# Adding the three taps of a depthwise convolution with accumulating DMA transfers instead of vector adds

## Chip, cores, metric

One core of a Trainium2 chip. The metric is device time in microseconds (us), median of several executions; the executions of one kernel agree within 0.3% to 1.5%. Engines: PE (matrix), DVE (vector), ACT (scalar activation), POOL (GpSimd), SP (queue for transfers).

## What is computed

The reference, cut to what matters. `B=2, T=16000, D=512`, all bfloat16:

```python
z = zeros_like(x)
for i in range(3):                       # depthwise conv over time, rounded to bf16 after each add
    z = z + xp[:, i:i+T, :] * dw_enc[i]
z = silu(z); res = z
for s in range(4):                       # residual quantizer, 8 codes per stage
    d2 = res.res - 2*res.cb + cb.cb;  idx = d2.argmin(-1)
    q = q + cb[idx];  res = res - cb[idx]
y = second depthwise conv of q with dw_dec
```

The two sums of the first convolution are each rounded. The kernel reproduces that rounding, because an argmin follows.

## The kernel before

Time is cut into 18 tiles of 1792 rows; D is cut into 4 chunks of 128. So a *chunk* below is one 128x1792 block, 4 per tile. A *tap* is one of the three products of a chunk, a *gate* the last DVE instruction of its front, and a transfer has *landed* when its completion is signalled to those who wait for it. Every tile passes four stages (front, select, residual, back), and stages of different tiles are interleaved. The parts that matter here:

```python
def load(st):                            # 14 transposing transfers per tile, SP queue, 2 buffers XT
    for g in list(range(G)):
        nc.sync.dma_start_transpose(out=X[:, :, g + 1, :], in_=src[g])
    ...
def taps(st, i):                         # chunk i: three products, two rounded adds, exponential
    for k in range(K):
        t = ppool.tile([P, R], BF16, name=f"P{k}")          # 3 buffers each
        nc.vector.tensor_scalar(out=t, in0=X[...k...], scalar1=WENC[:, i, k:k + 1], op0=ALU.mult)
        pk.append(t)
    nc.vector.tensor_tensor(out=pk[0], in0=pk[0], in1=pk[1], op=ALU.add)
    nc.vector.tensor_tensor(out=pk[0], in0=pk[0], in1=pk[2], op=ALU.add)
    nc.scalar.activation(pk[1], pk[0], ACT.Exp, scale=-1.0)
def plus1(st, i): ...                    # DVE +1, then ACT Ln and ACT Exp: 1/(1+exp(-z))
def gate(st, i): ...                     # DVE: z * sigmoid(z) into ZB (3 buffers)
...
def update(st, s, i, u, on_act):         # 24 per tile: residual minus chosen codes, in PSUM
    ... matmuls ...
    if on_act: nc.scalar.copy(zg, v)                       # 18 of 24
    else:      nc.vector.tensor_tensor(out=zg, in0=zg, in1=v, op=ALU.add)   # 6 of 24
...
def store(st): ...                       # one whole-tile output buffer, stores issued from GpSimd
```

The text gives a program order. The build step then chooses the order of instructions on each engine (the *built order*).

Of the kernel before, what the change touches and what calls it, by code (L numbers as in the profile page):

```python
# [8 lines left out]
BF16 = mybir.dt.bfloat16  # L9
F32 = mybir.dt.float32  # L10
U16 = mybir.dt.uint16
ALU = mybir.AluOpType
ACT = mybir.ActivationFunctionType
# [4 lines left out]
def kernel(  # L18
# [13 lines left out]
    nc = tc.nc  # L32
    P = nc.NUM_PARTITIONS
# [4 lines left out]
    KT = D // P  # L38
# [12 lines left out]
    const = ctx.enter_context(tc.tile_pool(name="const", bufs=1))  # L51
    ppool = ctx.enter_context(tc.tile_pool(name="ppool", bufs=3))
    lpool = ctx.enter_context(tc.tile_pool(name="lpool", bufs=2))
    selp = ctx.enter_context(tc.tile_pool(name="selp", bufs=2))
    small = ctx.enter_context(tc.tile_pool(name="small", bufs=3))
    ypool = ctx.enter_context(tc.tile_pool(name="ypool", bufs=2))
    psA = ctx.enter_context(tc.tile_pool(name="psA", bufs=3, space=bass.MemoryType.PSUM))
# [7 lines left out]
    make_identity(nc, IDENT)  # L65
    ONES = const.tile([P, P], BF16, name="ONES")
    nc.vector.memset(ONES, 1.0)

# [6 lines left out]

    WENC_b = const.tile([P, KT, K], BF16, name="WENC_b")
    WDBC = const.tile([P, K, D], BF16, name="WDBC")

    CB4 = const.tile([P, D], BF16, name="CB4")
    CB1 = const.tile([NC, D], BF16, name="CB1")  # L80
    wd_rows = bass.AP(tensor=dw_dec.tensor, offset=dw_dec.offset, ap=[[0, P], [D, K], [1, D]])
# [11 lines left out]

    CBT = const.tile([P, KT, NC], BF16, name="CBT")
    CBM2 = const.tile([P, KT, NC], BF16, name="CBM2")
    for i in range(KT):
# [23 lines left out]
    for i in range(KT):  # L120
        nc.tensor.matmul(pg[0:NC, 0:NC], lhsT=CBT[:, i, :], rhs=CBT[:, i, :],
                         start=(i == 0), stop=(i == KT - 1))
    GR = const.tile([NC, NC], F32, name="GR")
    nc.vector.tensor_copy(GR, pg[0:NC, 0:NC])
    NPART = 3
    GP = const.tile([NC, NPART, NC], BF16, name="GP")
    GREM = const.tile([NC, NC], F32, name="GREM")
    nc.vector.tensor_copy(GP[:, 0, :], GR)
# [7 lines left out]
    CCB = const.tile([P, 1, NC], BF16, name="CCB")  # L136
    CCD = const.tile([NC, NPART, NC], BF16, name="CCD")
    nc.vector.tensor_tensor(out=CCD, in0=GP, in1=IDENT[0:NC, 0:NC].rearrange("p (o c) -> p o c", o=1).to_broadcast([NC, NPART, NC]),
# [8 lines left out]

    GM = const.tile([GC, G, 1], F32, name="GM")
    nc.vector.tensor_reduce(out=GM[:, :, 0], in_=IDENT[0:GC, 0:GC].rearrange("p (g c) -> p g c", c=C), axis=AX.X, op=ALU.add)
    BD = {}  # L150
    for s in range(2):
        SEL = const.tile([NC, G, C], BF16, name=f"SEL{s}")
        nc.vector.tensor_copy(SEL, IDENT[0:NC, s * C:(s + 1) * C].rearrange("p (o c) -> p o c", o=1).to_broadcast([NC, G, C]))
        RP = const.tile([GC, NPART, NC], F32, name=f"RP{s}")
        pr = psS.tile([P, 512], F32, name="pr", tag="pss")
        nc.tensor.matmul(pr[0:GC, 0:NPART * NC], lhsT=SEL.rearrange("p g c -> p (g c)"),
                         rhs=GP.rearrange("p q c -> p (q c)"), start=True, stop=True)
        nc.vector.tensor_scalar(out=RP.rearrange("p q c -> p (q c)"), in0=pr[0:GC, 0:NPART * NC], scalar1=2.0,
                                scalar2=None, op0=ALU.mult)
        for s2 in range(s + 1, 3):  # L160
            for q in range(NPART):
                t = const.tile([GC, G, C], BF16, name=f"BD{s}_{s2}_{q}")
                nc.vector.tensor_tensor(out=t, in0=RP[:, q:q + 1, s2 * C:(s2 + 1) * C].to_broadcast([GC, G, C]),
                                        in1=GM.to_broadcast([GC, G, C]), op=ALU.mult)
                BD[s, s2, q] = t
# [4 lines left out]
    for j in range(4):  # L170
        t = const.tile([P, 1], F32, name=f"JM{j}")
        nc.vector.tensor_reduce(out=t, in_=idv[:, :, j, :], axis=AX.XY, op=ALU.add)
        JM.append(t)
# [3 lines left out]
    for v, tp in enumerate(((0, 1, 2, None), (None, 0, 1, 2), (None, None, 0, None), (None, 2, None, None))):  # L177
        w = const.tile([P, D], BF16, name=f"WDEC{v}")
        acc = None
        for j, k in enumerate(tp):  # L180
            if k is None:
                continue
            t = const.tile([P, D], BF16, name=f"WJ{j % 2}")
            nc.vector.tensor_scalar(out=t, in0=WDBC[:, k, :], scalar1=JM[j], scalar2=None, op0=ALU.mult)
            if acc is not None:
                nc.vector.tensor_tensor(out=t, in0=t, in1=acc, op=ALU.add)
            acc = t
        nc.vector.tensor_tensor(out=w, in0=CB4, in1=acc, op=ALU.mult)
        WDEC.append(w)

    CBN = {}
    for s in range(3):
        for u in range(2):
# [5 lines left out]
            CBN[s, u] = w  # L199

    NOH = 4
    PADC = 2
# [5 lines left out]
    for t in KEY:  # L208
        k16 = t.bitcast(U16).rearrange("p g (c h) -> p g c h", h=2)
        for c in range(C):  # L210
            nc.gpsimd.memset(k16[:, :, c, 0], c)


# [18 lines left out]
    def taps(st, i):  # L232
        X = XT[st["n"] % NX]
        pk = []
        for k in range(K):
            t = ppool.tile([P, R], BF16, name=f"P{k}")
            nc.vector.tensor_scalar(out=t, in0=X[:, i, k:k + G, :].rearrange("p g c -> p (g c)"),
                                    scalar1=WENC[:, i, k:k + 1], scalar2=None, op0=ALU.mult)
            pk.append(t)
        nc.vector.tensor_tensor(out=pk[0], in0=pk[0], in1=pk[1], op=ALU.add)  # L240
        nc.vector.tensor_tensor(out=pk[0], in0=pk[0], in1=pk[2], op=ALU.add)  # L241
        nc.scalar.activation(pk[1], pk[0], ACT.Exp, scale=-1.0)  # L242
        st["pk", i] = pk

    def plus1(st, i):
        pk = st["pk", i]
        nc.vector.tensor_scalar(out=pk[1], in0=pk[1], scalar1=1.0, scalar2=None, op0=ALU.add)
        LN = lpool.tile([P, R], F32, name="LN")
        nc.scalar.activation(LN, pk[1], ACT.Ln)
        nc.scalar.activation(pk[1], LN, ACT.Exp, scale=-1.0)  # L250

    def gate(st, i):
        pk = st["pk", i]
        Z = ZB[st["n"] % NZ]
        nc.vector.tensor_tensor(out=Z[:, i, :, N3:N3 + P], in0=pk[0].rearrange("p (g c) -> p g c", c=P),  # L255
                                in1=pk[1].rearrange("p (g c) -> p g c", c=P), op=ALU.mult)

# [113 lines left out]
    def update(st, s, i, u, on_act):  # L371
# [13 lines left out]
        else:  # L385
            nc.vector.tensor_tensor(out=zg, in0=zg, in1=v, op=ALU.add)  # L386

    def decode(st, k):
        W = OHW[st["n"] % NOH]
        if k == 0:  # L390
            st["Y"] = ypool.tile([P, G, D], BF16, name="Y")
        Y = st["Y"]
        py = psA.tile([P, 1024], F32, name="py", tag="psa")
        for u in range(2):
# [5 lines left out]
            elif wrap:  # L400
                nc.tensor.matmul(o, lhsT=W[:, 0, PADC + 1:PADC + 1 + P], rhs=WDEC[3], start=False, stop=True)
        nc.scalar.copy(Y[:, 2 * k:2 * k + 2, :].rearrange("p g d -> p (g d)"), py)  # L402
        if k == GH - 1:
            store(st)

    def store(st):

# [3 lines left out]
        for p in range(P):  # L411
            lo = max(a - G * p, 0)
            hi = min(e - G * p, G)
            if lo >= hi:
                continue
            if runs and runs[-1][2:] == [lo, hi]:
                runs[-1][1] = p + 1
            else:
                runs.append([p, p + 1, lo, hi])
# [4 lines left out]
        for p0, p1, lo, hi in split:  # L424
            nc.gpsimd.dma_start(out=view[p0:p1, lo:hi, :], in_=Y[p0:p1, lo:hi, :])  # L425


    def front(st):
        for j in range(KT + 2):
            if j < KT:  # L430
                yield lambda j=j: taps(st, j)
            if 1 <= j <= KT:
                yield lambda j=j: plus1(st, j - 1)
            if j >= 2:
                yield lambda j=j: gate(st, j - 2)

# [9 lines left out]
    def resid(st):  # L446
        m = 0
        for s in range(3):
            for u in range(2):
                for i in range(KT):  # L450
                    yield lambda s=s, i=i, u=u, m=m: update(st, s, i, u, m % 4 != 3)
                    m += 1
# [10 lines left out]
    NT = len(tiles)  # L463
    order = []
    for n, st in enumerate(tiles):
        order.append((n - 1.0, 0, lambda st=st: load(st)))
        for off, dur, gen in ((0.0, 1.0, front), (1.05, 0.55, select), (1.6, 1.0, resid), (2.6, 0.8, back)):
            w = list(gen(st))
            order += [(n + off + dur * (j + 0.5) / len(w), off, f) for j, f in enumerate(w)]
    for _, _, f in sorted(order, key=lambda t: t[:2]):  # L470
# [31 lines left out]
```

## Time and profile before

| | before |
|---|---|
| median | 889.0 us (887.43 to 890.19) |
| busy | DVE 739.6, ACT 736.1, PE 631.2 of 888.2 us |
| distance of two tiles (first gate to first gate) | 44.3 us |
| busy per period of 44.3 us | ACT 40.75, DVE 39.97, PE 34.97 |

The page's first part (engine, busy us, share of the span, x instructions) and the head of its chain that ended last:

```profile
span 888.2 us, 12372 instructions
...
PE 631.2 (71%) x4660; PEld 358.7 (40%) x4711; DVE 739.6 (83%) x1526; ACT 736.1 (83%) x667; POOL 79.7 (9%) x143
...
q1 hardware_dynamic: 137088, 33.06, 21.7%
q0 software_dynamic: 3840, 32.77, 11.8%
...
DVE 39%; ACT 29%; PE 22%; issue 5%; SPq 3%; DMA 1%; ACTq 0%; POOL 0%; POOLq 0%; DVEq 0%
```

The q lines are queues: packets, MB, share of the time of 16 DMA engines. Here q1 is the loads and q0 the stores. Hardly any of the chain is DMA.

Three consecutive periods of the kernel before, cut at first gates. Columns are in the first line:

```profile
core 0: us, PE busy (x) PEld busy (x) DVE busy (x) ACT busy (x) POOL busy (x), PEclk, DMA share, GB/s
296.60:340.90 44.30, 34.94 (x260) 19.75 (x261) 40.04 (x81) 40.73 (x38) 4.11 (x6) 0.92 0.39 84
340.90:385.30 44.40, 35.04 (x262) 19.89 (x263) 39.87 (x82) 40.82 (x38) 4.29 (x6) 0.92 0.40 84
385.30:429.60 44.30, 34.93 (x260) 19.73 (x261) 40.01 (x81) 40.71 (x38) 3.52 (x6) 0.92 0.39 84
```

Two engines are over 90% busy in every period, and about 3.6 us per period are lost. The DVE timeline (start us, length us) shows what an add and a DVE update cost when the engine is full, 1.00 us from start to start:

```profile
414.33 1.07 DVE L240 TENSOR_TENSOR P_4146<-P_4146,P_4148 128x1792 bf16<-128x1792 bf16 x1
415.33 1.07 DVE L386 TENSOR_TENSOR ZB_138<-ZB_138,pu 128x896 bf16<-128x896 bf16 x1
416.33 1.08 DVE L241 TENSOR_TENSOR P_4146<-P_4146,P_4150 128x1792 bf16<-128x1792 bf16 x1
```

### The profile page before, as it was taken

The numbers are of one execution on the slowest core, as the hardware profiler recorded it, in microseconds if no ns is written. First come the engines' busy times: TensorE is split into PE (matmuls) and PEld (weight loads), VectorE is DVE, ScalarE is ACT, GpSimd is POOL, SyncE is SP. The second block draws the span as 40 slices with busy tenths as digits, with TensorE's granted clock in tenths as the row PEclk, the third lists the DMA queues.
The fourth block names the chain that finished last, engine by engine and source line by source line (L and its number), as shares of the span: only waits on it lengthen the run. The fifth ranks groups of instructions, "written<-read, shape, count | busy, mean of one in ns | idle before, by whom it ended". The sixth has DMA issues, their size and how long they took to land.

```text
span 888.2 us, 12372 instructions
## 1 busy us (share of the span) xinstructions
PE 631.2 (71%) x4660; PEld 358.7 (40%) x4711; DVE 739.6 (83%) x1526; ACT 736.1 (83%) x667; POOL 79.7 (9%) x143
## 2 busy tenths in 40 slices
PE   1003587878787877777878787878787878778892
PEld 0002253535353535353535353535353535444540
DVE  4499999898989898989898989898989898984731
ACT  0076797989898989898989898989898989997572
POOL 5000000101010101010101010101010100000000
PEclk9998698989898989898989898989898989999997
DMA  4412322343434343434343534333534342020213
GB/s 96 95 30 59 78 46 39 94 74 92 75 94 73 96 71 97 70 100 67 99 68 99 68 97 66 103 65 100 67 99 67 98 69 78 7 84 1 84 51 112
DMA packets 143021, 67.20 MB, mean 76 GB/s; under 512 B 139932, under 2 KB 140572, under 8 KB 140700
## 3 DMA queue, kind: packets, MB, share of 16 engines
q1 hardware_dynamic: 137088, 33.06, 21.7%
q0 software_dynamic: 3840, 32.77, 11.8%
q10 hardware_dynamic: 2032, 0.56, 0.3%
q8 instruction: 37, 0.61, 0.3%
q14 instruction: 24, 0.20, 0.1%
HBM read 0.56 MB, written 32.77 MB: 38 GB/s over the span
## 4 chain that ended last, share of the span: by engine, by line
DVE 39%; ACT 29%; PE 22%; issue 5%; SPq 3%; DMA 1%; ACTq 0%; POOL 0%; POOLq 0%; DVEq 0%
PE pu L380 9%; PE pu L379 7%; ACT ZB_139 L384 6%; ACT ZB_137 L384 5%; ACT Y L402 5%; ACT ZB_138 L384 5%; SPq L228 3%; DVE ZB_137 L255 2%; DVE ZB_138 L255 2%; DVE ZB_139 L255 2%; PE pgr L270 2%; PE py L397 2%; DVE M L324 1%; DVE ZB_138 L386 1%; DVE ZB_139 L386 1%
## 5 line engine op out<-in xcount | busy, mean ns | idle before, releaser
L402 ACT CAST Y<-py 128x1024 bf16<-128x1024 f32 x126 | 130.6, 1043 | 13.8 <-PE py L397 13.8
L384 ACT CAST ZB_138<-pu 128x896 bf16<-128x896 f32 x108 | 95.9, 932 | 18.5 <-PE pu L380 18.0
L384 ACT CAST ZB_139<-pu 128x896 bf16<-128x896 f32 x108 | 95.6, 933 | 17.2 <-PE pu L380 16.7
L384 ACT CAST ZB_137<-pu 128x896 bf16<-128x896 f32 x108 | 95.7, 935 | 10.5 <-PE pu L380 10.5
L379 PEld LDWEIGHTS <-IDENT 128*128 128x128 bf16 x648 | 65.6, 101 | 77.8 <-issue 18.9
L270 PE MATMUL pgr<-ZB_137 128*128 128x152 bf16 (+1 forms) x672 | 56.4, 232 | 50.7 <-DVE ZB_137 L255 47.7
L379 PE MATMUL pu<-ZB_137,IDENT 128*128 128x512 bf16 (+1 forms) x216 | 81.1, 375 | 9.3 <-ACT ZB_137 L384 8.2
L379 PE MATMUL pu<-ZB_138,IDENT 128*128 128x512 bf16 x216 | 80.6, 373 | 7.8 <-ACT ZB_138 L384 6.7
L379 PE MATMUL pu<-ZB_139,IDENT 128*128 128x512 bf16 x216 | 80.1, 371 | 8.3 <-ACT ZB_139 L384 7.0
L267 PE MATMUL pgr<-MSK,IDENT 128*128 128x456 bf16 (+3 forms) x180 | 61.0, 339 | 23.2 <-ACT ZB_137 L384 4.8
L270 PEld LDWEIGHTS <-ZB_137 128*128 128x128 bf16 x672 | 48.4, 101 | 70.3 <-DVE ZB_137 L255 52.3
L288 DVE TENSOR_REDUCE rr<-pgr 128x6 f32<-128x768 f32 (+1 forms) x54 | 41.9, 775 | 36.2 <-PE pgr L270 36.1
L425 POOL DMA_DIRECT2D out_dram<-Y x66 | 34.1, 521 | 389.6 <-ACT Y L402 389.3
L386 DVE TENSOR_TENSOR ZB_139<-ZB_139,pu 128x896 bf16<-128x896 bf16 x36 | 39.1, 1085 | 27.9 <-PE pu L380 27.7
L386 DVE TENSOR_TENSOR ZB_138<-ZB_138,pu 128x896 bf16<-128x896 bf16 x36 | 39.0, 1083 | 20.5 <-PE pu L380 20.2
L270 PE MATMUL pgr<-ZB_139 128*128 128x152 bf16 (+1 forms) x672 | 53.3, 226 | 3.0 <-ACT ZB_139 L384 2.9
L270 PE MATMUL pgr<-ZB_138 128*128 128x152 bf16 (+1 forms) x672 | 53.6, 226 | 2.5 <-ACT ZB_138 L384 2.5
L270 PEld LDWEIGHTS <-ZB_139 128*128 128x128 bf16 x672 | 46.6, 98 | 18.4 <-issue 9.1
L270 PEld LDWEIGHTS <-ZB_138 128*128 128x128 bf16 x672 | 46.6, 98 | 17.7 <-issue 8.9
L386 DVE TENSOR_TENSOR ZB_137<-ZB_137,pu 128x896 bf16<-128x896 bf16 x36 | 39.0, 1084 | 12.1 <-PE pu L380 11.8
L242 ACT ACTIVATE P_348<-P_346 128x1792 bf16<-128x1792 bf16 x1 | 1.7, 1696 | 43.6 <-DVE P_346 L241 43.6
L380 PEld LDWEIGHTS <-CBN_0_262 128*128 128x128 bf16 x144 | 18.9, 131 | 32.6 <-issue 25.3
(1280 smaller groups left out, 1741.0 us busy)
## 6 DMA issues: line engine op xcount, KB each, us to landing
out_dram<-Y POOLq DMA_DIRECT2D x18, 1568.0 KB, 8.5
out_dram<-Y POOLq DMA_DIRECT2D x14, 196.0 KB, 8.2
XT_164<-in_x_dram SPq DMA_TRANSPOSE x126
XT_165<-in_x_dram SPq DMA_TRANSPOSE x126
out_dram<-Y POOLq DMA_DIRECT2D x30, 12.0 KB, 2.1
out_dram<-Y POOLq DMA_DIRECT2D x2, 210.0 KB, 8.9
WDBC<-in_dw_dec_dram ACTq DMA_DIRECT2D x1, 384.0 KB
CB_94<-in_codebooks_dram ACTq DMA_DIRECT2D x16, 8.0 KB
```

The costliest lines, as they stand in the source:

```text
L228: nc.sync.dma_start_transpose(out=X[:, :, g + 1, :], in_=src[g])
L255: nc.vector.tensor_tensor(out=Z[:, i, :, N3:N3 + P], in0=pk[0].rearrange("p (g c) -> p g c", c=P), in1=pk[1].rearrange("p (g c) -> p g c", ...
L267: nc.tensor.matmul(o, lhsT=IDENT, rhs=MSK[:, 0:nb, c0:c1], start=True, stop=False)
L270: nc.tensor.matmul(o[:, u * w:(u + 1) * w], lhsT=Z[:, i, b0 + u, N3:N3 + P], rhs=Z[:, i, b0 + u, c0:c1], start=False, stop=(u == nb - 1 an ...
L288: nc.vector.tensor_reduce(out=grp(st["rr"], g0, g1)[:, :, :, 0], in_=v[:, :, :, N3:N3 + P], axis=AX.X, op=ALU.max)
L379: nc.tensor.matmul(o, lhsT=IDENT, rhs=zg[:, k0:k0 + nk, :], start=True, stop=False)
L380: nc.tensor.matmul(o, lhsT=CBN[s, u][:, i * P:(i + 1) * P], rhs=W[:, k0:k0 + nk, PADC:PADC + P], start=not on_act, stop=True)
L384: nc.scalar.copy(zg, v)
L386: nc.vector.tensor_tensor(out=zg, in0=zg, in1=v, op=ALU.add)
L397: nc.tensor.matmul(o, lhsT=W[:, k, PADC:PADC + P], rhs=WDEC[u], start=True, stop=not wrap)
L402: nc.scalar.copy(Y[:, 2 * k:2 * k + 2, :].rearrange("p g d -> p (g d)"), py)
L425: nc.gpsimd.dma_start(out=view[p0:p1, lo:hi, :], in_=Y[p0:p1, lo:hi, :])
```

## The change

Intent: take the 8 adds per tile off DVE by letting DMA engines add in SBUF, and use the room on DVE to take 4 of the 18 updates off ACT. To make the latency of two transfers bearable, the front gets more stages in the program (`LAG`, in tiles) and more product buffers (`NB`); the memory comes from freeing setup tensors and from output buffers of 8 row groups instead of 14. Stores move from GpSimd to SP.

```diff
+    BYDMA = (1, 2)
+    NB = (5, 3, 4, 3)                       # buffers of P0, P1, P2, E
+    LAG = (0.01, 0.16, 0.31, 0.41, 0.42, 0.60)
...
         for k in range(K):
-            t = ppool.tile([P, R], BF16, name=f"P{k}")
+            t = ppool.tile([P, R], BF16, name=f"P{k}", bufs=NB[k])
...
-        nc.vector.tensor_tensor(out=pk[0], in0=pk[0], in1=pk[1], op=ALU.add)
-        nc.vector.tensor_tensor(out=pk[0], in0=pk[0], in1=pk[2], op=ALU.add)
-        nc.scalar.activation(pk[1], pk[0], ACT.Exp, scale=-1.0)
+    def add(st, i, k):
+        if k in BYDMA:
+            nc.gpsimd.dma_start(out=pk[0], in_=pk[k], accum_op=ALU.add)
+        else:
+            nc.vector.tensor_tensor(out=pk[0], in0=pk[0], in1=pk[k], op=ALU.add)
+    def expo(st, i):
+        E = ppool.tile([P, R], BF16, name="E", bufs=NB[3])
+        nc.scalar.activation(E, pk[0], ACT.Exp, scale=-1.0)
...
+    NDVE = 10
+    YG = 8
-                    yield lambda ...: update(st, s, i, u, m % 4 != 3)
+                    yield lambda ...: update(st, s, i, u, (m + 1) * NDVE // 24 == m * NDVE // 24)
...
-            nc.gpsimd.dma_start(out=view[p0:p1, lo:hi, :], in_=Y[p0:p1, lo:hi, :])
+            nc.sync.dma_start(out=view[p0:p1, g0 + lo:g0 + hi, :], in_=Y[p0:p1, lo:hi, :])
...
+            t = n + 0.25 * i
+            put(t, taps, st, i)
+            put(t + LAG[0], add, st, i, 1)
+            put(t + LAG[1], add, st, i, 2)
+            put(t + LAG[2], expo, st, i)
+            put(t + LAG[3], plus1, st, i)
+            put(t + LAG[4], inverse, st, i)
+            put(t + LAG[5], gate, st, i)
```

More of the change, by code (lines that the diff above doesn't have):

```diff
@@ L51 @@
     const = ctx.enter_context(tc.tile_pool(name="const", bufs=1))
-    ppool = ctx.enter_context(tc.tile_pool(name="ppool", bufs=3))
-    lpool = ctx.enter_context(tc.tile_pool(name="lpool", bufs=2))
-    selp = ctx.enter_context(tc.tile_pool(name="selp", bufs=2))
-    small = ctx.enter_context(tc.tile_pool(name="small", bufs=3))
-    ypool = ctx.enter_context(tc.tile_pool(name="ypool", bufs=2))
+    setup_pool = tc.tile_pool(name="setup", bufs=1)
+    setup = setup_pool.__enter__()
     psA = ctx.enter_context(tc.tile_pool(name="psA", bufs=3, space=bass.MemoryType.PSUM))
@@ L65 @@
     make_identity(nc, IDENT)
-    ONES = const.tile([P, P], BF16, name="ONES")
+    ONES = setup.tile([P, P], BF16, name="ONES")
     nc.vector.memset(ONES, 1.0)
@@ L74 @@
                                 op0=ALU.mult, op1=ALU.add)
-    WENC_b = const.tile([P, KT, K], BF16, name="WENC_b")
-    WDBC = const.tile([P, K, D], BF16, name="WDBC")
-    CB4 = const.tile([P, D], BF16, name="CB4")
-    CB1 = const.tile([NC, D], BF16, name="CB1")
+    WENC_b = setup.tile([P, KT, K], BF16, name="WENC_b")
+    WDBC = setup.tile([P, K, D], BF16, name="WDBC")
+    CB4 = setup.tile([P, D], BF16, name="CB4")
+    CB1 = setup.tile([NC, D], BF16, name="CB1")
     wd_rows = bass.AP(tensor=dw_dec.tensor, offset=dw_dec.offset, ap=[[0, P], [D, K], [1, D]])
@@ L91 @@
     nc.vector.tensor_copy(WENC, WENC_b)
-    CBT = const.tile([P, KT, NC], BF16, name="CBT")
-    CBM2 = const.tile([P, KT, NC], BF16, name="CBM2")
+    CBT = setup.tile([P, KT, NC], BF16, name="CBT")
+    CBM2 = setup.tile([P, KT, NC], BF16, name="CBM2")
     for i in range(KT):
@@ L122 @@
                          start=(i == 0), stop=(i == KT - 1))
-    GR = const.tile([NC, NC], F32, name="GR")
+    GR = setup.tile([NC, NC], F32, name="GR")
     nc.vector.tensor_copy(GR, pg[0:NC, 0:NC])
     NPART = 3
-    GP = const.tile([NC, NPART, NC], BF16, name="GP")
-    GREM = const.tile([NC, NC], F32, name="GREM")
+    GP = setup.tile([NC, NPART, NC], BF16, name="GP")
+    GREM = setup.tile([NC, NC], F32, name="GREM")
     nc.vector.tensor_copy(GP[:, 0, :], GR)
@@ L136 @@
     CCB = const.tile([P, 1, NC], BF16, name="CCB")
-    CCD = const.tile([NC, NPART, NC], BF16, name="CCD")
+    CCD = setup.tile([NC, NPART, NC], BF16, name="CCD")
     nc.vector.tensor_tensor(out=CCD, in0=GP, in1=IDENT[0:NC, 0:NC].rearrange("p (o c) -> p o c", o=1).to_broadcast([NC, NPART, NC]),
@@ L144 @@
     nc.vector.tensor_copy(CCB[:, 0, :], pc[:, 0:NC])
-    GM = const.tile([GC, G, 1], F32, name="GM")
+    GM = setup.tile([GC, G, 1], F32, name="GM")
     nc.vector.tensor_reduce(out=GM[:, :, 0], in_=IDENT[0:GC, 0:GC].rearrange("p (g c) -> p g c", c=C), axis=AX.X, op=ALU.add)
@@ L151 @@
     for s in range(2):
-        SEL = const.tile([NC, G, C], BF16, name=f"SEL{s}")
+        SEL = setup.tile([NC, G, C], BF16, name=f"SEL{s}")
         nc.vector.tensor_copy(SEL, IDENT[0:NC, s * C:(s + 1) * C].rearrange("p (o c) -> p o c", o=1).to_broadcast([NC, G, C]))
-        RP = const.tile([GC, NPART, NC], F32, name=f"RP{s}")
+        RP = setup.tile([GC, NPART, NC], F32, name=f"RP{s}")
         pr = psS.tile([P, 512], F32, name="pr", tag="pss")
@@ L170 @@
     for j in range(4):
-        t = const.tile([P, 1], F32, name=f"JM{j}")
+        t = setup.tile([P, 1], F32, name=f"JM{j}")
         nc.vector.tensor_reduce(out=t, in_=idv[:, :, j, :], axis=AX.XY, op=ALU.add)
@@ L182 @@
                 continue
-            t = const.tile([P, D], BF16, name=f"WJ{j % 2}")
+            t = setup.tile([P, D], BF16, name=f"WJ{j % 2}")
             nc.vector.tensor_scalar(out=t, in0=WDBC[:, k, :], scalar1=JM[j], scalar2=None, op0=ALU.mult)
@@ L211 @@
             nc.gpsimd.memset(k16[:, :, c, 0], c)
+    setup_pool.__exit__(None, None, None)
+    ppool = ctx.enter_context(tc.tile_pool(name="ppool", bufs=3))
+    lpool = ctx.enter_context(tc.tile_pool(name="lpool", bufs=2))
+    selp = ctx.enter_context(tc.tile_pool(name="selp", bufs=2))
+    small = ctx.enter_context(tc.tile_pool(name="small", bufs=3))
+    ypool = ctx.enter_context(tc.tile_pool(name="ypool", bufs=2))
     tiles = []
@@ L239, in taps, with inverse @@
             pk.append(t)
-        nc.vector.tensor_tensor(out=pk[0], in0=pk[0], in1=pk[1], op=ALU.add)
-        nc.vector.tensor_tensor(out=pk[0], in0=pk[0], in1=pk[2], op=ALU.add)
-        nc.scalar.activation(pk[1], pk[0], ACT.Exp, scale=-1.0)
         st["pk", i] = pk
+    def add(st, i, k):
+        pk = st["pk", i]
+        if k in BYDMA:
[3 more added lines that the diff above has]
+    def expo(st, i):
+        pk = st["pk", i]
+        E = ppool.tile([P, R], BF16, name="E", bufs=NB[3])
+        nc.scalar.activation(E, pk[0], ACT.Exp, scale=-1.0)
+        st["E", i] = E
     def plus1(st, i):
-        pk = st["pk", i]
-        nc.vector.tensor_scalar(out=pk[1], in0=pk[1], scalar1=1.0, scalar2=None, op0=ALU.add)
+        E = st["E", i]
+        nc.vector.tensor_scalar(out=E, in0=E, scalar1=1.0, scalar2=None, op0=ALU.add)
+    def inverse(st, i):
+        E = st["E", i]
         LN = lpool.tile([P, R], F32, name="LN")
-        nc.scalar.activation(LN, pk[1], ACT.Ln)
-        nc.scalar.activation(pk[1], LN, ACT.Exp, scale=-1.0)
+        nc.scalar.activation(LN, E, ACT.Ln)
+        nc.scalar.activation(E, LN, ACT.Exp, scale=-1.0)
     def gate(st, i):
-        pk = st["pk", i]
         Z = ZB[st["n"] % NZ]
-        nc.vector.tensor_tensor(out=Z[:, i, :, N3:N3 + P], in0=pk[0].rearrange("p (g c) -> p g c", c=P),
-                                in1=pk[1].rearrange("p (g c) -> p g c", c=P), op=ALU.mult)
+        nc.vector.tensor_tensor(out=Z[:, i, :, N3:N3 + P], in0=st["pk", i][0].rearrange("p (g c) -> p g c", c=P),
+                                in1=st["E", i].rearrange("p (g c) -> p g c", c=P), op=ALU.mult)
     def gram(st, g0, g1, c0, c1):
@@ L386, in update @@
             nc.vector.tensor_tensor(out=zg, in0=zg, in1=v, op=ALU.add)
+    NDVE = 10
+    YG = 8
     def decode(st, k):
         W = OHW[st["n"] % NOH]
-        if k == 0:
-            st["Y"] = ypool.tile([P, G, D], BF16, name="Y")
+        if 2 * k % YG == 0:
+            st["Y"] = ypool.tile([P, YG, D], BF16, name="Y")
         Y = st["Y"]
@@ L401, in decode, with store @@
                 nc.tensor.matmul(o, lhsT=W[:, 0, PADC + 1:PADC + 1 + P], rhs=WDEC[3], start=False, stop=True)
-        nc.scalar.copy(Y[:, 2 * k:2 * k + 2, :].rearrange("p g d -> p (g d)"), py)
-        if k == GH - 1:
-            store(st)
-    def store(st):
+        h = 2 * k % YG
+        nc.scalar.copy(Y[:, h:h + 2, :].rearrange("p g d -> p (g d)"), py)
+        if h == YG - 2 or k == GH - 1:
+            store(st, 2 * k - h, 2 * k + 2)
+    def store(st, g0, g1):
         Y, r0, a, e = st["Y"], st["row0"], st["a"], st["e"]
@@ L411, in store @@
         for p in range(P):
-            lo = max(a - G * p, 0)
-            hi = min(e - G * p, G)
+            lo = max(a - G * p, g0) - g0
+            hi = min(e - G * p, g1) - g0
             if lo >= hi:
@@ L424, in store @@
         for p0, p1, lo, hi in split:
-            nc.gpsimd.dma_start(out=view[p0:p1, lo:hi, :], in_=Y[p0:p1, lo:hi, :])
-    def front(st):
-        for j in range(KT + 2):
-            if j < KT:
-                yield lambda j=j: taps(st, j)
-            if 1 <= j <= KT:
-                yield lambda j=j: plus1(st, j - 1)
-            if j >= 2:
-                yield lambda j=j: gate(st, j - 2)
+            nc.sync.dma_start(out=view[p0:p1, g0 + lo:g0 + hi, :], in_=Y[p0:p1, lo:hi, :])
     def select(st):
@@ L450, in resid @@
                 for i in range(KT):
-                    yield lambda s=s, i=i, u=u, m=m: update(st, s, i, u, m % 4 != 3)
+                    yield lambda s=s, i=i, u=u, m=m: update(st, s, i, u, (m + 1) * NDVE // 24 == m * NDVE // 24)
                     m += 1
@@ L464, with put @@
     order = []
+    def put(t, f, *args):
+        order.append((t, len(order), lambda: f(*args)))
     for n, st in enumerate(tiles):
-        order.append((n - 1.0, 0, lambda st=st: load(st)))
-        for off, dur, gen in ((0.0, 1.0, front), (1.05, 0.55, select), (1.6, 1.0, resid), (2.6, 0.8, back)):
+        put(n - 1.0, load, st)
+        for i in range(KT):
+            t = n + 0.25 * i
[6 more added lines that the diff above has]
+            put(t + LAG[5], gate, st, i)
+        t = n + 0.75 + LAG[5] + 0.05
+        for dur, gen in ((0.55, select), (1.0, resid), (0.8, back)):
             w = list(gen(st))
-            order += [(n + off + dur * (j + 0.5) / len(w), off, f) for j, f in enumerate(w)]
+            for j, f in enumerate(w):
+                put(t + dur * (j + 0.5) / len(w), f)
+            t += dur
     for _, _, f in sorted(order, key=lambda t: t[:2]):
```

## The prediction

> **What bounds it now.** The busy table gives DVE 739.6 us (83%), ACT 736.1 (83%), PE 631.2 (71%) of 888.2. One tile of 18 passes every 44.3 us (first gates of tiles 3 and 4 start at 163.7 and 207.9 us). By the windows between 225 and 675 us, a period has ACT busy about 40.7 us, DVE 40.0, PE 35. So ACT and DVE bound together; about 3.5 us per period go in hand-overs (chain of waits: DVE 39%, ACT 29%, PE 22%). Some 135 us are fill and drain.
>
> **What the change does, per tile.**
> - 8 DVE adds of 128x1792 leave (1.08 us each in the line listing, 1.00 start to start in the timeline): DVE -8.0 us.
> - Residual updates on DVE go from 6 to 10 of 24: DVE +4.0 (1.00 each, start to start); ACT loses 4 casts of 0.93 us (0.87 start to start): -3.5; PE loses 8 identity matmuls of 0.37: -3.
> - Sum: DVE 40.0 to 36.0, ACT 40.7 to 37.2, PE 35 to 32.
> - 8 accumulating transfers of 448 KB, 144 in all. The Trainium skill ("DMA: Bandwidth & Descriptors", "SWDGE vs HWDGE vs iDMA") says that only GpSimd can issue accumulation; it states no rate, and this trace has none. My estimate: stores moved 32.77 MB in 11.8% of 16 engines' span, 313 GB/s; an accumulation reads two streams, so 2 x 459 KB / 313 GB/s = 2.9 us, plus the 2.1 us to landing of the 12 KB stores: 5 us each. DMA share goes from 34% to 80%. Program order leaves 0.15 tile (6 us) for each: just hidden.
> - Transposes (20 us per tile from release to landing) slow down, perhaps to 30 us, and have about one period: still hidden.
> - Stores move from GpSimd to SP in two parts: the last is smaller, about 3 us less at the end.
> - GpSimd issues 8 transfers per tile instead of 3.7. The skill ("SBUF — State Buffer", "SBUF: two separate sides") says that DVE in a two-port mode and GpSimd lock each other out of a shared port. Here, single taps took 1.08 us instead of 0.67 beside a GpSimd copy. I allow 0.5 us per tile.
> - Gates come 0.35 tile later in program order: +8 to +12 us of fill and drain.
>
> **On the critical path.** ACT stays the busiest engine, so the period shrinks by its 3.5 us, to 40.8 with hand-overs as before. 17 x 3.5 = 59 us less, +10 for fill and drain, -3 for the last store: 889 - 52 = 837 us. Range 812 to 872. Chances: faster 0.84, same 0.09, slower 0.07.
>
> **What would show each step.** First gates 40.8 us apart; ACT and DVE each about 670 us busy, PE about 580; no adds in the taps on DVE; 144 accumulating transfers landing in 4 to 7 us; DMA share 70 to 85%; little of DVE's or ACT's idle time ended by DMA.
>
> **What would make it wrong.** An accumulation several times slower than a copy: above about 5 us of engine time each, 8 of them with loads and stores exceed the period, the exponentials on ACT wait for the second transfer, and DMA binds (950 us or more). GpSimd's queue is in order and waits for the first sum before it issues the second: with a landing above 9 us each pair passes a quarter of a period. Or descriptor writing stalls DVE's taps by over 2 us per tile. The other way, smaller hand-over losses, since all three engines have more slack, would bring 820.

## The result

1088.86 us against 888.25 us for the kernel before on the same chip (4 runs each): ratio 1.2273, 95% interval 1.2209 to 1.2337. The result is correct. A ratio here is the mean time of one kernel's runs over the mean of the other's of the same rounds, so it is not quite the ratio of the medians quoted. Executions over 1.5% slower than the fastest of the same kernel are left out of the means.

The page of the changed kernel, same parts as before. q0 is now the accumulating transfers, q1 loads and stores:

```profile
span 1088.3 us, 12320 instructions
...
PE 645.9 (59%) x4516; PEld 373.8 (34%) x4567; DVE 680.5 (63%) x1454; ACT 679.3 (62%) x595; POOL 167.9 (15%) x221
...
q0 software_dynamic: 20736, 66.07, 34.8%
q1 hardware_dynamic: 142760, 65.83, 29.1%
...
DMA 31%; DVE 28%; issue 14%; PE 11%; SPq 9%; ACT 4%; POOL 2%; ACTq 0%; POOLq 0%; DVEq 0%
```

Three of its periods, columns as before:

```profile
596.30:651.20 54.90, 36.95 (x253) 21.75 (x259) 36.54 (x78) 37.56 (x33) 8.51 (x10) 0.88 0.67 134
651.20:705.60 54.40, 36.50 (x253) 20.63 (x256) 36.41 (x77) 37.80 (x33) 8.50 (x10) 0.87 0.68 134
705.60:760.30 54.70, 36.91 (x253) 21.58 (x259) 36.57 (x77) 37.56 (x33) 8.50 (x10) 0.88 0.66 135
```

The work did fall as predicted: DVE 36.5 us per period (predicted 36.0), ACT 37.6 (predicted 37.2). But a period is 54.7 us, so ACT stands still for 17 us of it and DVE for 18. The DMA engines are not full either: their share is 0.67.

The first gates show where the 200 us lie. Before, they run from 55.7 to 783.0 us, after from 83.3 to 974.2. So the 17 periods cost 890.9 instead of 727.3 us (+164), the fill 28 us more, and the stretch behind the last tile's first gate 9 us more (114.1 instead of 105.2).

Where does DVE stand? Its timeline over 20 us of the changed kernel; the bracket is the idle time before an instruction and what ended it. Line 244 is a tap, 406 an update, 275 a gate:

```profile
548.48 0.68 DVE L244 TENSOR_SCALAR P_4553<-XT_152,WENC 128x1792 bf16<-128x1792 bf16 x1
...
549.61 0.68 DVE L244 TENSOR_SCALAR P_4676<-XT_152,WENC 128x1792 bf16<-128x1792 bf16 x1
550.20 0.68 DVE L244 TENSOR_SCALAR P_4786<-XT_152,WENC 128x1792 bf16<-128x1792 bf16 x1
550.80 1.08 DVE L406 TENSOR_TENSOR ZB_126<-ZB_126,pu 128x896 bf16<-128x896 bf16 x1
554.87 0.69 DVE L244 TENSOR_SCALAR P_4951<-XT_153,WENC 128x1792 bf16<-128x1792 bf16 x1 [2.99 <-DMA P_4553<-P_4555]
555.47 1.08 DVE L406 TENSOR_TENSOR ZB_126<-ZB_126,pu 128x896 bf16<-128x896 bf16 x1
559.04 0.69 DVE L244 TENSOR_SCALAR P_5038<-XT_153,WENC 128x1792 bf16<-128x1792 bf16 x1 [2.49 <-DMA P_4676<-P_4678]
559.64 1.08 DVE L406 TENSOR_TENSOR ZB_126<-ZB_126,pu 128x896 bf16<-128x896 bf16 x1
...
567.02 0.69 DVE L244 TENSOR_SCALAR P_5162<-XT_153,WENC 128x1792 bf16<-128x1792 bf16 x1 [2.76 <-DMA P_4676<-P_4680]
567.63 1.09 DVE L275 TENSOR_TENSOR ZB_125<-P_4303,E 128x1792 bf16<-128x1792 bf16 x1
569.49 0.69 DVE L244 TENSOR_SCALAR P_5271<-XT_153,WENC 128x1792 bf16<-128x1792 bf16 x1 [0.77 <-DMA P_4786<-P_4790]
```

Read it so. Three chunks get their first product together (P_4553, P_4676, P_4786), so six accumulating transfers run in a bunch. Right behind them in DVE's list stand taps of the *next* tile: P_4951 is the second product of a chunk whose P1 buffer is still being read by the transfer P_4553<-P_4555. The tap may write only when that transfer has landed. Updates and the gate stand behind the waiting tap, and PE and ACT wait for those in turn: between 240 and 640 us DVE is idle for 135 us, 82 of them for such landings; ACT never waits for a landing there, but 62 us for PE's part of the updates and 49 us for gates. Only P0 buffers are freed by a gate; P1 and P2 buffers are freed by a landing.

One chunk's life, from the instructions that write or read its first product (at the line's end: first and last start):

```profile
L244 DVE TENSOR_SCALAR P_4553<-XT_152,WENC x1: 680/680/680, 548.5 to 548.5; 128x1792 bf16<-128x1792 bf16 x1
L253 POOL DMA_DIRECT2D P_4553<-P_4555 x1: 1269/1269/1269, 549.7 to 549.7; - x1
L253 POOL DMA_DIRECT2D P_4553<-P_4557 x1: 859/859/859, 555.1 to 555.1; - x1
L260 ACT ACTIVATE E<-P_4553 x1: 1701/1701/1701, 573.6 to 573.6; 128x1792 bf16<-128x1792 bf16 x1
L275 DVE TENSOR_TENSOR ZB_126<-P_4553,E x1: 1092/1092/1092, 598.9 to 598.9; 128x1792 bf16<-128x1792 bf16 x1
```

The program gives it 0.60 tile from tap to gate; it took 50 us. The next bunch of first products starts at 603.5, after the gates of P_4466, P_4553 and P_4676 (596.3 to 599.9) have freed three P0 buffers. The loop is: gates free P0 buffers, three taps, six landings with DVE waiting through them, late updates, late gates.

The 144 transfers landed after 7.5 us in the median (4.2 to 19.6), by the listing of issues. The longest ones are in the fill, beside loads. The first transfers of the three chunks above, issued together, and one issued alone afterwards (KB, us to landing):

```profile
P_4553<-P_4555 POOLq DMA_DIRECT2D x1, 448.0 KB, 5.1
P_4676<-P_4678 POOLq DMA_DIRECT2D x1, 448.0 KB, 8.2
P_4786<-P_4788 POOLq DMA_DIRECT2D x1, 448.0 KB, 9.5
...
P_4949<-P_4951 POOLq DMA_DIRECT2D x1, 448.0 KB, 4.9
```

The second and third of a bunch land late; one alone takes 4.9 us.

### The profile page after: what moved, and what is told of

It is laid out like the page before. It is cut to its first block, busy times and chain, and to the rows that moved or that the text cites. A ratio compares the mean times of both kernels' runs of the same rounds, so it can differ in the third digit from the quotient of the medians.

```text
span 1088.3 us, 12320 instructions
## 1 busy us (share of the span) xinstructions
PE 645.9 (59%) x4516; PEld 373.8 (34%) x4567; DVE 680.5 (63%) x1454; ACT 679.3 (62%) x595; POOL 167.9 (15%) x221
## 3 DMA queue, kind: packets, MB, share of 16 engines
q0 software_dynamic: 20736, 66.07, 34.8%
## 4 chain that ended last, share of the span: by engine, by line
DMA 31%; DVE 28%; issue 14%; PE 11%; SPq 9%; ACT 4%; POOL 2%; ACTq 0%; POOLq 0%; DVEq 0%
SPq L235 9%; PE pgr L290 4%; PE pu L400 3%; DVE ZB_125 L406 3%; DVE ZB_126 L406 2%; DVE E L265 2%; DVE ZB_127 L406 2%; DMA P_387<-P_389 2%; DVE ZB_126 L275 1%; PE pu L399 1%; DVE rr L308 1%; DVE ZB_125 L275 1%; DVE ZB_127 L275 1%; DMA P_4303<-P_4307 1%; ACT Y L426 1%
## 5 line engine op out<-in xcount | busy, mean ns | idle before, releaser
L270 ACT ACTIVATE LN<-E 128x1792 f32<-128x1792 bf16 x72 | 122.7, 1707 | 41.5 <-DVE E L265 41.5
L271 ACT ACTIVATE E<-LN 128x1792 bf16<-128x1792 f32 x72 | 122.1, 1701 | 0.4
L290 PE MATMUL pgr<-ZB_125 128*128 128x152 bf16 (+1 forms) x672 | 63.9, 249 | 92.3 <-DVE ZB_125 L275 91.1
L399 PEld LDWEIGHTS <-IDENT 128*128 128x128 bf16 x504 | 52.0, 103 | 166.3 <-DVE S L309 104.4
L404 ACT CAST ZB_126<-pu 128x896 bf16<-128x896 f32 x84 | 74.9, 918 | 49.3 <-PE pu L400 45.0
L404 ACT CAST ZB_125<-pu 128x896 bf16<-128x896 f32 x84 | 74.4, 912 | 47.3 <-PE pu L400 42.7
L399 PE MATMUL pu<-ZB_125,IDENT 128*128 128x512 bf16 (+1 forms) x168 | 66.5, 396 | 57.7 <-DVE S L309 36.1
L399 PE MATMUL pu<-ZB_126,IDENT 128*128 128x512 bf16 (+1 forms) x168 | 64.5, 385 | 55.5 <-DVE S L309 31.0
L404 ACT CAST ZB_127<-pu 128x896 bf16<-128x896 f32 x84 | 74.6, 916 | 33.6 <-PE pu L400 32.9
L290 PEld LDWEIGHTS <-ZB_125 128*128 128x128 bf16 x672 | 55.7, 110 | 106.7 <-DVE ZB_125 L275 96.0
L399 PE MATMUL pu<-ZB_127,IDENT 128*128 128x512 bf16 (+1 forms) x168 | 63.3, 378 | 39.5 <-DVE S L309 23.5
L287 PE MATMUL pgr<-MSK,IDENT 128*128 128x456 bf16 (+3 forms) x180 | 72.6, 404 | 2.1 <-DVE MSK L70 1.8
L406 DVE TENSOR_TENSOR ZB_127<-ZB_127,pu 128x896 bf16<-128x896 bf16 x60 | 65.0, 1083 | 13.1 <-PE pu L400 12.8
L406 DVE TENSOR_TENSOR ZB_125<-ZB_125,pu 128x896 bf16<-128x896 bf16 x60 | 64.9, 1081 | 8.8 <-PE pu L400 8.6
L406 DVE TENSOR_TENSOR ZB_126<-ZB_126,pu 128x896 bf16<-128x896 bf16 x60 | 64.9, 1081 | 5.9 <-PE pu L400 5.4
L290 PE MATMUL pgr<-ZB_127 128*128 128x152 bf16 (+1 forms) x672 | 67.0, 258 | 1.0 <-DVE ZB_127 L406 0.7
L290 PE MATMUL pgr<-ZB_126 128*128 128x152 bf16 (+1 forms) x672 | 65.1, 253 | 1.5 <-DVE ZB_126 L406 1.0
L290 PEld LDWEIGHTS <-ZB_127 128*128 128x128 bf16 x672 | 59.5, 116 | 12.1 <-issue 6.7
L290 PEld LDWEIGHTS <-ZB_126 128*128 128x128 bf16 x672 | 57.1, 112 | 11.8 <-issue 5.0
L265 DVE TENSOR_SCALAR E<-E 128x1792 bf16<-128x1792 bf16 x72 | 46.4, 645 | 4.2 <-ACT E L260 4.2
```

The source lines that it names most:

```text
L265: nc.vector.tensor_scalar(out=E, in0=E, scalar1=1.0, scalar2=None, op0=ALU.add)
L270: nc.scalar.activation(LN, E, ACT.Ln)
L271: nc.scalar.activation(E, LN, ACT.Exp, scale=-1.0)
L287: nc.tensor.matmul(o, lhsT=IDENT, rhs=MSK[:, 0:nb, c0:c1], start=True, stop=False)
L290: nc.tensor.matmul(o[:, u * w:(u + 1) * w], lhsT=Z[:, i, b0 + u, N3:N3 + P], rhs=Z[:, i, b0 + u, c0:c1], start=False, stop=(u == nb - 1 an ...
L399: nc.tensor.matmul(o, lhsT=IDENT, rhs=zg[:, k0:k0 + nk, :], start=True, stop=False)
```

## Experiments

Theory A: the landings are waited for by engines that execute in order, because the built order puts taps (and exponentials) where the landing has not come yet. Rival B: bytes; accumulation and transposes together are more than the DMA engines can move in a period. Rival C: the rest of the rewrite (stores in SP's queue, longer front).

Every run below was timed in 3 rounds. "DVE for landings" and "ACT for landings" are my sums of the idle times ended by an accumulating transfer that the timelines list between 240 and 640 us of each run. A zero means none is listed; short ones are not listed.

| run | us | ratio to before | landing, median us | DVE for landings | ACT for landings |
|---|---|---|---|---|---|
| changed kernel | 1089 | 1.227 | 7.5 | 82 | 0 |
| e1 both adds on DVE | 914 | 1.029 | none | none | none |
| e2 one add by transfer | 960 | 1.079 | 5.0 | 0 | 0 |
| e3 64 of 1792 columns (wrong result) | 882 | 0.994 | 2.9 | 26 | 0 |
| f4 896 columns (wrong result) | 979 | 1.101 | 4.0 | 37 | 0 |
| e4 plain copy (wrong result) | 947 | 1.067 | 4.8 | 54 | 0 |
| e8 joint product buffer | 959 | 1.080 | 6.0 | 0 | 56 |
| e11 taps held | 999 | 1.124 | 4.7 | 0 | 84 |
| f1 e8 + longer lags | 976 | 1.098 | 5.1 | 0 | 49 |
| f2 longer lags alone | 1083 | 1.220 | 5.9 | 79 | 0 |
| f3 6 updates on DVE | 1105 | 1.246 | 6.3 | 76 | 0 |
| e13 taps and exponentials held | 1066 | 1.199 | 4.8 | 0 | 50 |
| e14 e13 + longer lags | 942 | 1.061 | 5.4 | 0 | 6 |
| g1 e14 with adds on DVE | 979 | 1.102 | none | none | none |
| **g2 joint buffer, longer lags, exponentials held** | **904** | **1.018** | 5.8 | 0 | 0 |

Not in the table: e5, e10, e17 and e18, told below.

### e1: the rest of the change without accumulating transfers

```diff
-    BYDMA = (1, 2)
+    BYDMA = ()
-    NDVE = 10
+    NDVE = 6
```

> Edit: the whole new kernel, but both adds on DVE again and 6 of 24 updates on DVE, as before; buffers, lags, half-tile outputs and stores from SP stay new. Theory A (DVE, in order, waits for landings of the accumulating transfers, because its taps reuse product buffers that a transfer still reads): no landings, so about 890 us (870 to 910), period 44 to 45 us. Rival C (the rest of the rewrite, above all stores ahead of loads in SP's queue and the longer front, costs the time): stays above 1000 us.

Measured 914 us, 2.9% over before (2.7 to 3.1), 4 us outside the expected range. So the transfers and what goes with them are 175 of the 200 us, and the rest of the rewrite costs 25 us that the prediction had only as 10 us of fill. Part of the run is remarkable; two windows of 40 us of e1, columns as before:

```profile
240.00:280.00 40.00, 30.64 (x241) 18.11 (x243) 39.92 (x82) 39.81 (x37) 0.74 (x1) 0.91 0.50 120
440.00:480.00 40.00, 29.57 (x217) 16.30 (x218) 34.14 (x72) 32.77 (x31) 2.37 (x2) 0.91 0.33 76
```

Between 240 and 280 us both DVE and ACT are full; later the same work settles into a period of 48 us with both at 85% or less. I take the built order, which settles into one pattern per period, for the reason; that was not isolated. In the profiled executions (911.6 against 888.2 us) its 17 periods cost 734.2 us together, only 7 more than before, as the first ones are short; 16 us of the loss lie behind the last tile's first gate (120.9 instead of 105.2), which the prediction did not foresee.

### e2: one add by transfer

```diff
-    BYDMA = (1, 2)
+    BYDMA = (2,)
```

> Edit: only the second add by transfer, the first on DVE; 10 updates on DVE as in the changed kernel. DVE work per tile is as before the change, ACT has 3.5 us less. Theory A: half of the landings, no pair in series, so DVE's wait for landings at most half (under 6 us per tile against 11), and 900 to 980 us. Rival B (bytes: accumulation and transposes saturate the DMA engines): landings fall near 5 us and the time near 870. Rival C: above 1000.

960 us, inside A's range, but not by A's route: between 240 and 640 us no wait of DVE for an accumulation is listed. Instead its taps wait 58 us there for loads and stores, and ACT's exponentials 62 us for gates. This run does not tell the theories apart.

### e3, f4 and e4: what a landing is worth

e3 and f4 shorten each transfer, keeping all 144 of them and all waits:

```diff
-            nc.gpsimd.dma_start(out=pk[0], in_=pk[k], accum_op=ALU.add)
+            nc.gpsimd.dma_start(out=pk[0][:, 0:64], in_=pk[k][:, 0:64], accum_op=ALU.add)      # e3; f4: 0:896
```

> Wrong result on purpose: each accumulating transfer adds 64 of 1792 columns; all 144 transfers and their waits stay, 1/28 of the bytes. The built order moves a little. Landing should be 2 to 3 us. If the time of the landing (transfer of bytes) is the cost (A or B): 840 to 880 us. If the mere chain of two transfers through GpSimd's in-order queue is the cost, or rival C: above 1000 us.

> Wrong result on purpose: each accumulating transfer adds 896 of 1792 columns, 224 KB. Landing alone about 3.8 us, between 2.9 (64 columns) and 4.8 (full, uncontended). If the loss follows the landing time: 930 to 1000. If it jumps where bunched transfers overlap: near 882 to 910.

e3: 882 us (2 us over the expected range), with landings of 2.9 us. Its settled periods are 42.5 us (44.4 before, means of twelve): with landings this short about half of the predicted 3.5 us appears, though DVE still loses 26 of 400 us to them. f4: 979 us, inside the range for a loss that follows the landing, with landings of 4.0 us. The number of transfers and GpSimd's queue are the same in all three, so they are not the cost; the loss grows with the length of the landing. The built order moves between these runs, so they are no pure measurement.

e4 has exactly the built order of the changed kernel, on every engine (the lists of all engines in the two traces agree instruction by instruction, semaphore waits left out):

```diff
-            nc.gpsimd.dma_start(out=pk[0], in_=pk[k], accum_op=ALU.add)
+            nc.gpsimd.dma_start(out=pk[0], in_=pk[k])
```

> Wrong result on purpose: the same transfers without accumulation (plain copies, same bytes, same issue, and the built order of all engines is the same). If the read-modify-write is what makes landings slow: landing 3 to 4 us, GpSimd queue share of the DMA engines from 35% to under 20%, and time 900 to 980. If latency and place in the order matter and not the accumulation: landing stays near 7 us and the time within 3% of 1089.

947 us, as forecast: 142 us less, for the same instructions in the same order. (The finer forecasts were missed: landings of 4.8 us instead of 3 to 4, and 22.1% of the engines instead of under 20%.) Its queue of copies and its issues (KB each, median us from issue to landing):

```profile
q0 software_dynamic: 11520, 66.07, 22.1%
...
P<-P POOLq DMA_DIRECT2D x144, 448.0 KB, 4.8
```

An accumulation takes 34.8% of 1088.3 us / 144 = 2.63 us of all 16 engines, a copy 22.1% of 946.2 us / 144 = 1.45 us. (The prediction's estimate for the accumulation was 2.9 us.) With the accumulation's longer occupation a bunch of six lands late: 7.5 us instead of 4.8. In the same order, that difference is 142 us. So neither the choice of engine nor the order alone is the loss; it is a landing time that this order does not tolerate.

### e8 and e11: freeing the buffers otherwise, holding the taps

e8 allocates the three products of a chunk together, so that no buffer is freed by a landing alone (12 product tiles as before):

```diff
-            t = ppool.tile([P, R], BF16, name=f"P{k}", bufs=NB[k])
+        PP = ppool.tile([P, K, R], BF16, name="PP", bufs=4)     # ahead of the loop; t = PP[:, k, :]
```

e11 leaves the buffers and only forbids that taps of a chunk stand ahead of the gate of the chunk three before it:

```diff
+        with (tc.issue_after(GATES[c - 3].ins) if c >= 3 else ExitStack()):
             for k in range(K): ...                              # the three taps
```

> Edit: the changed kernel, the three products of a chunk in one allocation of 4 buffers (same 12 product tiles): the second and third product are freed by the gate and not by a landing. Theory A: the taps stop waiting for landings, as in e11, time 880 to 980. If only bytes matter: above 1040. The fewer chunks in flight (4 instead of 5) may cost some.

> Edit: the changed kernel; only the order on DVE is held: the taps of a chunk may not stand before the gate of the chunk three before it, which is the program's own order. Same instructions, buffers and bytes. Theory A (order): taps no longer stand behind fresh landings, the transfers of a tile spread over it, landing median 5 to 6 us, DVE idle for landings under 4 us per tile (11 in the changed kernel), time 880 to 960. Theory B (bytes saturate the DMA engines): landing stays above 7 us, time above 1040.

e8: 959 us, as A said. e11: 999 us, between the two. In both, DVE's listed waits for landings are gone, from 82 us to zero, and in e11 the landings are back at 4.7 us with the DMA engines' bytes unchanged: with the 4.9 us of a lone transfer in the changed kernel, this says that bunching made them long, not the total. But a new wait appeared. The first exponential on ACT, which reads the finished sum, now stands ahead of its landing, and in e8 DVE stands 57 of 400 us at its +1, waiting for that exponential. Two of its instances in e8's timeline of ACT:

```profile
501.46 1.70 ACT L261 ACTIVATE E<-PP 128x1792 bf16<-128x1792 bf16 x1 [7.33 <-DMA PP<-PP]
...
547.78 1.70 ACT L261 ACTIVATE E<-PP 128x1792 bf16<-128x1792 bf16 x1 [5.83 <-DMA PP<-PP]
```

### f1, f2, f3: lags and the division of updates

```diff
-    LAG = (0.01, 0.16, 0.31, 0.41, 0.42, 0.60)
+    LAG = (0.01, 0.20, 0.50, 0.62, 0.63, 0.82)      # f2 in the changed kernel; f1 in e8
-    NDVE = 10
+    NDVE = 6                                        # f3, in the changed kernel
```

> Edit: e8 (959 us) with the lags of e14 and no held order. e8's remaining waits were ACT's exponentials for the second landing, 7 us per tile. If the place of the exponential in the program is what lets it stand before its landing: those waits fall under 3 us per tile and the time to 895 to 935. If the built order takes no notice of the lags: 950 to 970.

> Edit: the changed kernel with the lags of e14 alone. DVE's taps still wait for landings through the second and third product's buffers, so if those waits are the main cost: 1050 to 1100, DVE idle for landings over 8 us per tile. If the lags are: below 1000.

> Edit: the changed kernel with 6 of 24 updates on DVE as before the change (ACT gets 3.5 us per tile back, DVE loses 4). If updates behind stalled taps on DVE spread the stall to PE and ACT: 1000 to 1060. If the landings' own loop sets the period: within 2% of 1089, as neither DVE nor ACT is full.

f2, 1083 us, as forecast: longer lags alone gain 6 us. The built order moved with them (the list of DVE differs from the changed kernel's), but DVE still waits 79 us for landings. f1, 976 us: a miss of both forecasts, 17 us worse than e8; its ACT still waits 49 us for landings. f3, 1105 us, inside its 2%: giving the four updates back to ACT changes little, since neither engine is full. The shift of updates is not the fault.

### e13, e14, e17, e18, g1: holding the order on both engines

These hold the taps and the first exponential behind the instruction of another stage that precedes them in the program on their engine:

```diff
+        with (tc.issue_after(LAST["v"].ins) if "v" in LAST else ExitStack()):   # ahead of the three taps
+        with (tc.issue_after(LAST["a"].ins) if "a" in LAST else ExitStack()):   # ahead of the first exponential
```

> Edit: the changed kernel; the taps on DVE and the first exponential on ACT of each chunk are held behind the instruction of another stage that precedes them in the program on their engine. Buffers, lags and bytes unchanged. e11 held the taps alone, 999 us, and its wait moved to ACT's exponentials (10 us per tile for landings). Theory A (in-order engines stand before landings that the built order takes to come sooner): ACT's wait for landings under 4 us per tile, time 880 to 950. Rival B (the DMA engines, or GpSimd's chain of two transfers, cannot deliver faster): stays above 980.

> Edit: e13 with longer lags in the program (second transfer 0.20 instead of 0.16 tile after the taps, exponential 0.50 instead of 0.31, gate 0.82 instead of 0.60). Theory A: with 12 us left for each landing nothing waits for a transfer, DVE 36 and ACT 37 us per tile show through, period 41 to 43 us, time 850 to 900. Rival B: no better than e13.

> Edit: e1 (no accumulating transfers, 6 updates on DVE; 914 us) with the same holds as e13. If e1's 25 us over the kernel before are an accident of the built order: 870 to 895. If they come from the longer front and its buffers: 905 or more.

> Edit: e2 (second add by transfer, first on DVE, 10 updates on DVE; 960 us) with the same holds and lags 0.20, 0.40, 0.52, 0.72. DVE has 40 us of work per tile, ACT 37, one landing per chunk. Theory A: 870 to 900, DVE bound. Rival B: bytes half of e14, so clearly faster than e14 and near e2 or below.

> Edit: e14 with both adds on DVE and 6 updates on DVE; same holds and lags. Pair to e14 (942 us). If moving the adds gains once no engine waits for a landing (the prediction's sum of 3.5 to 4 us per tile): 985 to 1010. If the gain is not there: 935 to 955.

My forecasts failed here. e13 took 1066 us instead of 880 to 950; by its time alone that was rival B's forecast (above 980), which e14 then contradicts. e17, the same holds without any accumulating transfer, took 988 us: its second branch (905 or more), but the holds on both engines cost 74 us by themselves (914 without), so it does not say what e1's 25 us are. e18 took 987 us instead of 870 to 900. So theory A as I had it, "keep the program's order and the gain appears", is wrong: e13 gains only 23 us on the changed kernel, and the same holds cost 74 us where there is no landing to wait for.

e14 missed its forecast too (850 to 900). It and e13 differ in their lags alone: 942 against 1066 us, and ACT's waits for landings fall from 50 to 6 us. With the holds in force, the lags count. e14 and g1 have the same holds and lags and differ only in where the adds and four updates are done. One period of e14, then one of g1:

```profile
606.00:652.00 46.00, 34.04 (x254) 19.09 (x256) 35.85 (x77) 37.85 (x35) 8.59 (x10) 0.93 0.85 152
```

```profile
520.90:570.80 49.90, 36.59 (x258) 20.18 (x261) 40.93 (x82) 40.54 (x38) 2.17 (x2) 0.90 0.31 74
```

942 against 979 us, 3.9% apart by their ratios to before (1.0606 and 1.1024); 979 lies between g1's two forecasts, 6 us short of the one for a gain. With landings nearly hidden, the shift of work goes with a shorter period: 3.9 us in these two windows, 46.2 against 49.9 us in the mean of twelve, where the prediction had 3.5. (What the holds leave free of the built order may differ between the two.) It just starts from a worse kernel.

### g2: no landing in the way, DVE's order free

Joint buffer (e8), longer lags, and a hold on the exponential alone.

> Edit: e8's joint buffer, lags of e14, and only the exponential held behind the preceding ACT instruction of the program; DVE's order free. Theory A: ACT's waits for landings under 2 us per tile (7 in e8, 6 in f1), time 890 to 940. If a free DVE order again stands where it waits: 950 or more.

903.9 us, correct, ratio 1.018 (1.015 to 1.022). It fell in theory A's forecast. This is the best version that computes the result with both adds by transfer: all bytes, all 144 accumulations, 10 updates on DVE, and 185 us faster than the changed kernel. No wait of DVE or ACT for a landing is listed between 240 and 640 us. Three of its periods:

```profile
582.00:626.60 44.60, 32.88 (x254) 18.55 (x255) 36.98 (x77) 37.39 (x34) 8.75 (x10) 0.96 0.76 161
626.60:670.80 44.20, 32.94 (x253) 18.51 (x254) 36.50 (x77) 37.33 (x34) 9.42 (x11) 0.96 0.83 164
670.80:714.60 43.80, 32.81 (x253) 18.55 (x254) 36.07 (x76) 37.40 (x34) 8.86 (x10) 0.96 0.97 163
```

Rival B, that the total is too much, falls with it. The DMA engines' share is up to 0.97 of a period here, and the kernel is far faster than the changed one at 0.67. But no version that computes the result beats the kernel before (e3, which does not, is 0.6% faster): 6.8 us of every period are still lost (44.2 minus 37.4), nearly twice the 3.6 us of before. What ends the idle time is now ACT's Ln waiting for DVE's +1 (39 us between 240 and 640 us) and DVE and ACT waiting for PE's updates (37 and 19 us), so hand-overs between engines of one chain.

### e5 and e10: the stores

e5 is e1 with the stores issued from GpSimd again; e10 is the changed kernel with stores issued from ACT.

```diff
-            nc.sync.dma_start(out=view[...
+            nc.gpsimd.dma_start(out=view[...        # e5;  e10: nc.scalar.dma_start
```

> Edit: e1 (both adds on DVE, 6 updates on DVE) with the half-tile stores issued from GpSimd as before the change, SP has loads alone. e1 took 914 us. If the stores in SP's in-order queue make loads late (theory of e1's 25 us): 880 to 893, and DVE's taps no longer wait for loads or stores. If the longer front and its buffers cost it: 905 to 920.

> Edit: the changed kernel with the stores issued from ACT's queue, behind the copies that they wait for anyway; SP has loads alone. If stores in front of loads are a large part of the 200 us: below 1040. If they are only what e1 showed: 1050 to 1085, with the waits for landings unchanged.

e5 took 928.6 us, worse than e1 and outside both ranges; e10 took 1176 us, outside both too. Moving the stores away from SP's queue gave nothing back in either, so stores in front of loads are not shown to cost anything; e5 is the fair test of the two, as in e10 ACT has the stores in its own list. Why e10 is that much worse was not followed: DVE waits 83 of 400 us for landings, as much as in the changed kernel; its periods vary between 48 and 77 us once it is under way, and the built order changed with the edit.

## Why the prediction was wrong

- **What bounds the kernel, and the work moved: right.** DVE 36.5 and ACT 37.6 us per period against 36.0 and 37.2 predicted; in all 680.5 and 679.3 us against "about 670". PE was 646 instead of 580 us; its matmuls were slower than before in the record (232 to 249 ns for one group of score matmuls) at a granted clock of 0.88 instead of 0.92.
- **Cost of one accumulation: right within 10%.** 2.63 us of 16 engines against 2.9 estimated, and 4.7 us to landing where transfers are spread (e11) against 5.
- **DMA share of 80%: not reached in the changed kernel** (0.67), because its periods are too long; g2, with the same bytes in 44 us, shows 0.76 to 0.97.
- **GpSimd's descriptor writing: no visible harm.** All 216 taps took 0.69 us in the mean before and after; the longest was 1.08 us before and 0.92 after. The Trainium skill ("SBUF — State Buffer", "SBUF: two separate sides") states the lock between GpSimd and DVE; by these durations its cost stayed within the 0.5 us per tile allowed. That only GpSimd can issue an accumulation was taken from the page that the prediction names; no run here tests it.
- **The step that failed: "Program order leaves 0.15 tile (6 us) for each: just hidden."** The kernel does not run in program order, so nothing reserved these 6 us. The built order puts DVE's taps of the next tile right behind the transfers that free their buffers, and bunches three chunks. Bunched, the median landing was 7.5 us, and DVE, in order, lost 82 of 400 us to it, with updates, PE and ACT behind it. The wait that the prediction did not have is that of a tap for a *source* buffer which a transfer still reads; it had only the wait for the finished sum. Speeding up the landings in the same order gave 142 us (e4); removing the waits on both engines gave 185 us (g2).
- **"40.8 with hand-overs as before": failed too, even with landings hidden.** g2 loses 6.8 us per period instead of 3.6. That is 3.2 x 17 = 54 us of the 67 us between the predicted 837 and its 904. By first gates all 67 are there: its 17 periods took 735.5 us, 8 more than before where 59 less were predicted, while fill (+9.7 us) and drain (-4.1) came as predicted. Why is open. A settled order with as few gaps as the old one was not found. That e1 has such gaps too (periods of 48 us without any accumulation) suggests that they belong to the new front and its built order rather than to the transfers; this was not shown.
- **What I had named as risks** was not what came: not over 5 us of engine time for one accumulation (2.63), not a landing over 9 us in the median, not stalled descriptors.

Settled: the landings and the waits of in-order engines for them make up most of the 200 us (175 by e1, 142 by e4 in the same order, 185 by g2); the total of bytes does not bind the changed kernel. Open: the larger hand-over losses of the new front, and the exact share of the order in e1.

## What to carry to other kernels

Work moved to transfers has to land before an in-order list reaches whatever waits for it, and a buffer freed by a landing counts as such a wait just as data does: look for what recycles it. Here that was needed, and still not enough (g2). Lags written into the program did not keep instructions from their waits where the build was free to reorder (f2); read the order on each engine in the timeline, and test with the same order and a faster transfer before blaming bandwidth. Taking 8% of the busy time off both bounding engines gave nothing here, because the lost time between them grew by more.

## What the Trainium skill lacked or had wrong

- "DMA: Bandwidth & Descriptors", section "SDMA does more than copy", lists addition in the DMA engines without a rate, and no page has one for an accumulation inside one core's SBUF. Here a 448 KB bfloat16 accumulation took 2.63 us of 16 engines, a plain copy of the same bytes 1.45 us; 20736 / 144 = 144 packets against 80.
- The same page's fit for one transfer, section "Anatomy of one DMA", is 2.0 us + bytes / 436 GB/s. For 458,752 bytes that makes an estimate of 3.1 us, for 16 KB 2.0. The fastest plain copies of e4 and 16 KB accumulations of e3 landed after 2.7 and 2.1 us, so the fit is not wrong; but beside loads, stores and each other the medians were 4.8 and 2.9 us, and the page has no figure for such company.
- The same page's rule to issue a transfer early and wait late ("Rules for kernel authors") is right but lacks the case that decided here: a compute instruction that reuses the *source* buffer waits for the landing too (82 of 400 us on DVE).
- No page gives landing times of accumulations issued in a bunch: 5.1, 8.2 and 9.5 us for three issued together, median 7.5 us (up to 19.6 in the fill), against 4.7 us when spread (e11).
